# A three-layer kernel with a hand-stored plan: halves of the solved triangle stored apart, two more key buffers, and a plan made anew

## The chip, the core and the metric

The kernel runs on one core of one Trainium2 chip. The metric is the device time of one execution in microseconds (us). The core has TensorE (matrix products; PE in the profile, its weight loads PEld), VectorE (DVE), ScalarE (ACT), GpSimd (POOL) and SyncE (SP), which here does nothing but issue transfers. Each engine works through its own instructions strictly in the order in which they were written, and waits on semaphores for the others.

## What is computed

Three layers on 3072 tokens of 384 channels, cut here to their core. The first is a linear attention whose state is corrected by what it already holds for a key (4 batches, 8 heads, 768 positions, 48 channels per head):

```
k_n = k / (norm(k) + 1e-6)
for t in range(S):
    y[t]  = q[t] @ state
    state = state + beta[t] * outer(k_n[t], v[t] - k_n[t] @ state)
```

The second sends each token with a positive skip score to one of 8 experts and adds gate * relu(x @ w1[e]) @ w2[e]. The third normalises by the root of the mean square and gives (silu(x @ w_gate) * (x @ w_val)) @ w_out.

## The kernel before

The 768 positions are handled in 12 chunks of 64, two to a group (groups 0 to 5); 64 of the partitions hold half of the batches, and a step for one chunk handles the rest in two streams (bp 0 and 1), each with its own state in a PSUM bank (banks 70 and 71 in the order below). Every f32 operand of a product is split into two f16 halves, high and low, and each product is three matmuls (high-high, low-high, high-low).

For each group, `norms` and `prepk` load the keys, normalise and split them (NK), copy them into the order that a turn by DMA needs (four transfers into NB, tag nb, on SP), turn them (KC, a transposing transfer), form the Gram matrices and store them to DRAM (gd). `solve` loads four 32 x 32 blocks per problem from gd, inverts them in 30 steps of two VectorE operations each (tags sm and sa), sets the diagonal (a memset, L271), scales the result (Ts), splits it into halves (Th, Tl) and stores it to DRAM twice, as it is (td) and turned (tn). `merge`, once for each chunk of the group, loads the blocks into W (eight transfers for the group's two chunks from td) and dn (four from tn), and builds the missing block of the 64 x 64 inverse on TensorE (z at L295, x at L310), with ScalarE writing the result into W (x1h, x1l). `prepq` turns the queries and forms their Gram matrix. `step` is the recurrence for one chunk and stream: split the state (Sh on ScalarE, Sl on VectorE with the state's bank as its source), form the residual with it (ks), multiply by W (u), update the state (S), and give the output (yq, y). A step can do ks without W; u needs it.

`Route` then projects each output tile for the experts and scatters the rows; `Rest` decodes and splits the weights of the gated layer, runs the experts and then the gated layer.

The order of the work is not found at run time. `Sched` collects some 3440 operations; `follow` gives each the place, the engine and the buffer slot that stand in three tables, ORDER_, ON_ and SLOT_; `emit` writes them out so. The cost numbers in `dma`, `conv` and the others are those from which a planner made the tables; they are not read when the kernel runs.

The interleaved layout of before: td is [block, problem, row, column, half], so that the high and the low of an element lie side by side, and W keeps that in its last axis.

Of the kernel before, what the change touches and what calls it, by code (L numbers as in the profile page):

```python
# [104 lines left out]
B,H,S,D=4,8,768,48  # L105
# [13 lines left out]
class Base:  # L119
# [58 lines left out]
class Attn(Base):  # L178
# [19 lines left out]
    def norms(s,g):  # L198
        nc=s.nc; sm=lambda: s.small.buf([32])
        n2=sm(); s.ksrc=[]  # L200
        for hf in range(2):
            kf=s.pk.buf([2,HD]); s.ksrc.append(kf)
            s.dma(lambda kf=kf: kf.ap,lambda hf=hf: s.I['kn'][g,hf].rearrange("p (q e)->p q e",q=2),393216,[],[kf],tag="ldk")
# [15 lines left out]
    def prepk(s,g):  # L219
# [3 lines left out]
        for hf in range(2):  # L223
# [7 lines left out]
            for u in range(2):  # L231
                for bp in range(2):
                    s.dma(lambda u=u,bp=bp,NB=NB: NB.ap[UH[bp],:,:,u].rearrange("p l h d->p (l h) d"),lambda u=u,bp=bp,NK=NK: NK.ap[UH[u],bp].rearrange("p l h d->p (l h) d"),260000,[NK],[(NB,(u,bp))],tag="nb")
            s.dma(lambda KC=KC: KC.ap.rearrange("p l h t->p (l h) t"),lambda NB=NB: NB.ap.rearrange("p l h u d->p (l h u d)"),524288,[NB],[KC],tag="trk",kind="t")
# [8 lines left out]
            s.dma(lambda hf=hf: gd.ap[:,16*hf:16*hf+16],lambda gs=gs: gs.ap.rearrange("p q h j->p (q h) j"),524288,[gs],[(gd,hf)],tag="gout")  # L243
# [6 lines left out]
    def solve(s,g):  # L250
# [5 lines left out]
        for b in range(4):  # L256
            half,u=b//2,b%2; r=64*u+32*half
            s.dma(lambda b=b: A.ap[32*b:32*b+32],lambda r=r,half=half: gd.ap[r:r+32,:,32*half:32*half+32].rearrange("i a j->a i j"),262144,[gd],[(A,("l",b))],tag="lda")
# [14 lines left out]
        td=Fixed(s.dram(f"td{g}",[4,32,32,32,2],F16)); tn=Fixed(s.dram(f"tn{g}",[2,32,32,32,2],F16)); s.td[g]=(td,tn)  # L273
        for o in range(2):
            n=(128,64)[o]; Th=s.pTh.buf([32,32,2],F16); src=(lambda: A.ap) if o==0 else (lambda: A.ap[0:64].rearrange("p c i->p i c"))
            s.conv(lambda Th=Th,n=n: Th.ap[0:n,:,:,0],src,1024,[A],[(Th,0)],tag="Th")
            s.tt(lambda Th=Th,n=n: Th.ap[0:n,:,:,1],src,lambda Th=Th,n=n: Th.ap[0:n,:,:,0],ALU.subtract,1024,[A,(Th,0)],[(Th,1)],tag="Tl")
            to=td if o==0 else tn
            s.dma(lambda to=to: to.ap.rearrange("b a r c l->(b a) (r c l)"),lambda Th=Th,n=n: Th.ap[0:n].rearrange("a r c l->a (r c l)"),4096*n,[Th],[to],tag="td")

    def merge(s,g,hf):
# [3 lines left out]
        W=s.pW.buf([2*H,2,32,2],F16); s.W[g,hf]=W; dn=s.pdn.buf([2*H,32,2],F16)  # L285
        R=[[slice(64*u+32*f,64*u+32*f+32) for f in range(2)] for u in range(2)]
        for u in range(2):
            for f in (1,0):
                s.dma(lambda u=u,f=f: W.ap[R[u][f],:,f].rearrange("p a c l->p a (c l)"),lambda u=u,f=f: td.ap[2*f+u,sa].rearrange("a r c l->r a (c l)"),90000,[td],[(W,(f,u))],tag="W")
            s.dma(lambda u=u: dn.ap[R[u][0]].rearrange("p a c l->p a (c l)"),lambda u=u: tn.ap[u,sa].rearrange("a r c l->r a (c l)"),90000,[tn],[(dn,u)],tag="dn")  # L290
        pz=s.ps.buf([2*H,32]); zw=s.pzw.buf([2,2*H,32],F16); fl=lambda a: a.rearrange("p a c->p (a c)")
        def zmm(e,bp):
            for a in range(H*bp,H*bp+H):
                for i,(x,y) in enumerate(((0,0),(1,0),(0,1))):
                    for u in range(2): nc.tensor.matmul(pz.ap[R[u][0],a],GB.ap[R[u][1],x,a],W.ap[R[u][1],a,1,:,y],start=a==0 and i==0,stop=a==2*H-1 and i==2,skip_group_check=True)  # L295
# [22 lines left out]
    def prepq(s,g,q):  # L318
        nc=s.nc; hf,bp=q//2,q%2
        if bp==0:  # L320
            qv=s.pqv.buf([2,2*HD])
            s.dma(lambda: qv.ap,lambda: s.I['qv'][g,hf].rearrange("p (x e)->p x e",x=2),786432,[],[qv],tag="ldq")
# [9 lines left out]
            s.dma(lambda: QC.ap.rearrange("p l h t->p (l h) t"),lambda: NQ.ap.rearrange("p l h d->p (l h d)"),524288,[NQ],[QC],tag="trq",kind="t")  # L332
# [27 lines left out]
    def step(s,g,q,QC,Pt):  # L360
# [19 lines left out]
        s.prod(lambda u,h: pu.ap[u,h],lambda u,l,h: W.ap[u,H*bp+h,:,:,l].rearrange("p f c->p (f c)"),rt,True,True,[W],Rh,pu,[Uh],"u")  # L380
# [141 lines left out]
class Rest(Base):  # L522
# [72 lines left out]
    def moe(s,S):  # L595
        nc=s.nc
        for e in range(E):
# [5 lines left out]
            s.dma(lambda xT=xT: xT.ap.rearrange("p b l k t->p (b l k) t"),lambda xh=xh: xh.ap.rearrange("p b l d->p (b l d)"),393216,[xh],[xT],tag="trx",kind="t")  # L603
# [24 lines left out]
    def glu(s):  # L628
        nc=s.nc
        t0=0  # L630
        for st,N in enumerate(GROUPS):
# [17 lines left out]
            for b in range(N):  # L649
# [3 lines left out]
                s.dma(lambda xT=xT,b=b: xT.ap[:,b].rearrange("p l k t->p (l k) t"),lambda xh=xh: xh.ap.rearrange("p l d->p (l d)"),196608,[xh],[(xT,b)],tag="trn",kind="t")  # L653
# [137 lines left out]
ORDER_=[21,17,33,24,36,168,226,6,9,19,81,34,20,22,35,18,1,37,3,5,4,38,2,169,0,23,14,7,39,170,8,29,12,30,227,10,40,13,41,80,11,25,42,228,26,171,43,16,238,44,32,28,264,45,172,27,46,173,31,47,  # L791
# [90 lines left out]
```

## Time and profile before

| | us |
|---|---|
| median of 3 runs | 1117.39 (1116.77 to 1117.95) |
| the profiled execution, its own time | 1119.22 |
| its span, first to last instruction | 1117.5 |
| busy: TensorE / VectorE / ScalarE | 873.7 / 654.1 / 376.0 |
| mean granted TensorE clock, share of full | 0.826 |

The span falls into attention (to about 505 us), the wait for the experts (to 528), the experts (to 661), a second wait (to 682) and the gated layer. TensorE is nearly always busy in the experts and the gated layer, at a granted clock of 0.98 to 0.99; in attention it works at 0.58 to 0.76, with pauses. Busy times of matmuls are modelled at their ends. A wait is put down to the one that ended last.

### The profile page before, as it was taken

What the parts mean: (1) busy time and instruction counts of PE and PEld (TensorE: products, weight loads), DVE (VectorE), ACT (ScalarE), POOL (GpSimd) and SP (SyncE); (2) the same over time, 40 slices, a digit from 0 to 9 for tenths busy, and PEclk for the clock granted to TensorE, in tenths of its full rate; (3) what the DMA queues carried; (4) which work ended last, traced back from release to release, by engine and by line L of the source; (5) the groups of instructions that cost most, each with busy time, mean ns of one, the idle gap of its engine ahead of it and who ended that gap; (6) DMA issues with size and microseconds to landing.
All of it is one profiled execution on the core that took longest, in us unless ns stands there. A gap on an engine that the chain in (4) does not pass through costs nothing.

```text
span 1117.5 us, 31866 instructions
## 1 busy us (share of the span) xinstructions
PE 873.7 (78%) x14102; PEld 596.9 (53%) x14102; DVE 654.1 (59%) x1511; ACT 376.0 (34%) x707; POOL 64.0 (6%) x83
## 2 busy tenths in 40 slices
PE   0320775975887769681999965999999999999996
PEld 0320564764775657561777745865454444545553
DVE  6458756677566666759989998753424353331230
ACT  3221343461534424451545415643131221111100
POOL 5000001001001010011000012211000000000000
PEclk9955576675666867665999986999999999999998
DMA  9992577386674851765899755531120101000000
GB/s 273 194 218 76 107 147 157 80 171 112 118 137 145 174 109 55 194 198 167 226 289 298 217 164 161 129 89 47 23 70 1 28 2 29 29 1 22 22 15 31
DMA packets 233154, 132.00 MB, mean 118 GB/s; under 512 B 199038, under 2 KB 214995, under 8 KB 233010
## 3 DMA queue, kind: packets, MB, share of 16 engines
q1 hardware_dynamic: 229938, 122.83, 45.1%
q0 software_dynamic: 3072, 7.07, 2.2%
q8 instruction: 112, 1.84, 0.7%
q14 instruction: 32, 0.26, 0.1%
HBM read 74.04 MB, written 31.46 MB: 94 GB/s over the span
## 4 chain that ended last, share of the span: by engine, by line
PE 60%; DMA 11%; DVE 10%; issue 8%; SPq 6%; ACT 4%; another core or an unknown queue 0%; POOL 0%; POOLq 0%; ACTq 0%; DVEq 0%
PE bank L160 14%; PE bank L166 8%; PE bank L168 8%; PE bank L167 8%; SPq L152 6%; PE bank L676 4%; PE bank L674 4%; PE bank L675 4%; DVE arena L136 3%; ACT arena L128 3%; DVE arena L134 3%; DMA arena<-in_w_dram 3%; DMA arena<-arena 3%; PE bank L310 2%; DMA arena<-yd,arena 1%
## 5 line engine op out<-in xcount | busy, mean ns | idle before, releaser
L134 DVE TENSOR_TENSOR arena<-arena 128x512 f16<-128x512 f32 (+20 forms) x558 | 257.7, 472 | 58.4 <-ACT arena L128 25.6
L160 PE MATMUL bank<-arena 64*64 64x48 f16 (+1 forms) x7776 | 197.5, 212 | 102.8 <-DMA arena<-arena 63.5
L166 PE MATMUL bank<-arena 128*128 128x512 f16 (+2 forms) x768 | 236.7, 316 | 42.0 <-DMA arena<-arena 39.2
L160 PEld LDWEIGHTS <-arena 64*64 64x64 f16 x7776 | 183.1, 134 | 132.5 <-issue 65.7
L167 PE MATMUL bank<-arena 128*128 128x512 f16 (+2 forms) x768 | 236.8, 316 | 0.2 <-issue 0.2
L168 PE MATMUL bank<-arena 128*128 128x512 f16 (+2 forms) x768 | 236.7, 316 | 0.0
L128 ACT ACTIVATE arena<-bank 128x384 f16<-128x384 f32 (+4 forms) x258 | 129.6, 529 | 312.5 <-PE bank L676 98.8
L128 ACT ACTIVATE arena<-arena 128x512 f16<-128x512 f32 (+6 forms) x187 | 138.4, 756 | 161.5 <-DVE arena L136 30.4
L136 DVE SCALAR_TENSOR_TENSOR arena<-arena 128x768 f16<-128x768 f32 (+4 forms) x163 | 136.8, 855 | 47.2 <-ACT arena L128 36.4
L136 DVE SCALAR_TENSOR_TENSOR arena<-arena,bank 128x512 f32<-128x512 f32 (+2 forms) x96 | 52.7, 552 | 148.7 <-PE bank L168 111.9
L167 PEld LDWEIGHTS <-arena 128*128 128x128 f16 x768 | 76.5, 100 | 88.9 <-issue 43.0
L664 ACT ACTIVATE arena<-bank 128x512 f32<-128x512 f32 (+2 forms) x96 | 46.2, 488 | 168.3 <-PE bank L168 127.4
L166 PEld LDWEIGHTS <-arena 128*128 128x128 f16 x768 | 76.5, 100 | 46.3 <-issue 0.3
L168 PEld LDWEIGHTS <-arena 128*128 128x128 f16 x768 | 76.5, 100 | 46.2 <-issue 0.3
L674 PE MATMUL bank<-arena 128*128 128x384 f16 x288 | 93.9, 326 | 0.0
L675 PE MATMUL bank<-arena 128*128 128x384 f16 x288 | 93.9, 326 | 0.0
L676 PE MATMUL bank<-arena 128*128 128x384 f16 x288 | 93.9, 326 | 0.0
L129 DVE CAST arena<-arena 128x512 f16<-128x512 f32 (+2 forms) x69 | 28.8, 417 | 58.1 <-PE bank L675 36.6
L295 PE MATMUL bank<-arena 32*32 32x32 f16 x1152 | 22.0, 183 | 42.9 <-DMA arena<-td 30.0
L517 POOL DMA_INDIRECT xs<-arena x24 | 24.4, 1017 | 475.5 <-DMA arena<-td 171.8
L136 DVE SCALAR_TENSOR_TENSOR arena<-bank,arena 128x256 f16<-128x256 f32 (+1 forms) x86 | 37.9, 453 | 13.7 <-ACT arena L128 11.4
L619 PE MATMUL bank<-arena 128*128 128x384 f16 x128 | 41.7, 326 | 2.7 <-DVE arena L130 1.4
(113 smaller groups left out, 735.8 us busy)
## 6 DMA issues: line engine op xcount, KB each, us to landing
arena<-in_w_dram SPq DMA_DIRECT2D x24, 512.0 KB
arena<-in_w_dram SPq DMA_DIRECT2D x32, 384.0 KB
arena<-in_qv_dram SPq DMA_DIRECT2D x12, 768.0 KB
arena<-arena SPq DMA_DIRECT2D x48, 128.0 KB
gd<-arena SPq DMA_DIRECT2D x12, 512.0 KB
arena<-in_kn_dram SPq DMA_DIRECT2D x12, 384.0 KB
xd<-arena SPq DMA_DIRECT2D x12, 384.0 KB
arena<-in_wg_dram SPq DMA_DIRECT2D x9, 512.0 KB
```

The costliest lines, as they stand in the source:

```text
L128: if e is s.nc.scalar: e.activation(out(),in_(),AF.Copy,scale=sc)
L134: return s.sch.op(alts,lambda e: e.tensor_tensor(out(),a(),b(),op=op),r=r,w=w,tag=tag,prio=prio)
L136: return s.sch.op([("DVE",0.07+n*0.00104,port)],lambda e: e.scalar_tensor_tensor(out(),a(),sc() if callable(sc) else sc,b(),op0=op0,op1=op ...
L152: else: fn=lambda e: e.dma_start(out(),in_())
L160: for u in UH: nc.tensor.matmul(o(u),l(u),r(u),start=first and i==0,stop=last and i==n-1,skip_group_check=True)
L166: nc.tensor.matmul(out,lh,rh,start=first,stop=False,skip_group_check=True)
L167: nc.tensor.matmul(out,ll,rh,start=False,stop=False,skip_group_check=True)
L168: nc.tensor.matmul(out,lh,rl,start=False,stop=last,skip_group_check=True)
L664: s.act(lambda e,sg=sg,pp=pp: e.activation(sg.ap,pp[0].ap,AF.Silu,scale=2.0**-7),T,[pp[0]],[sg],table="silu",tag="silu")
L674: nc.tensor.matmul(po.ap,hT.ap[:,f,0,bs],s.wo.ap[:,0,c],start=f==0,stop=False)
L675: nc.tensor.matmul(po.ap,hT.ap[:,f,0,bs],s.wo.ap[:,1,c],start=False,stop=False)
L676: nc.tensor.matmul(po.ap,hT.ap[:,f,1,bs],s.wo.ap[:,0,c],start=False,stop=f==11)
```

## The change

Three things. First, td, tn, Th, W and dn keep the high and the low half apart: in W the axes are now [problem, half, block, column], so that 32 columns of one half lie together. Matmuls and conversions read and write them without a stride; a load of W from td now moves runs of 32 f16 (64 bytes), 1024 of them, where it moved 512 runs of 128 bytes; a load of dn keeps its 128-byte runs. Second, KC (turned keys) and NK (normalised keys) have six slots each instead of five, and one more buffer is zeroed at the start. Third, the sizes and issue times of transfers in the planner's costs are other numbers, and the three tables are other tables, so that the order of the instructions differs nearly everywhere.

```diff
-        return s.sch.op([("SP",1.8 if kind=="t" else 0.46,0)],fn,r=r,w=w,kind=kind,nb=nb,tag=tag,prio=prio)
+        return s.sch.op([("SP",0.7+nb*1.6e-6 if kind=="t" else {"lda":0.61,"W":0.53,"nb":0.73}.get(tag,0.45),0)],fn,r=r,w=w,kind=kind,nb=nb,tag=tag,prio=prio)
...
-        td=Fixed(s.dram(f"td{g}",[4,32,32,32,2],F16)); tn=Fixed(s.dram(f"tn{g}",[2,32,32,32,2],F16)); s.td[g]=(td,tn)
+        td=Fixed(s.dram(f"td{g}",[4,32,2,32,32],F16)); tn=Fixed(s.dram(f"tn{g}",[2,32,32,2,32],F16)); s.td[g]=(td,tn)
...
-        W=s.pW.buf([2*H,2,32,2],F16); s.W[g,hf]=W; dn=s.pdn.buf([2*H,32,2],F16)
+        W=s.pW.buf([2*H,2,2,32],F16); s.W[g,hf]=W; dn=s.pdn.buf([2*H,2,32],F16)
...
-                s.dma(lambda u=u,f=f: W.ap[R[u][f],:,f].rearrange("p a c l->p a (c l)"),lambda u=u,f=f: td.ap[2*f+u,sa].rearrange("a r c l->r a (c l)"),90000,[td],[(W,(f,u))],tag="W")
+                s.dma(lambda u=u,f=f: W.ap[R[u][f],:,:,f].rearrange("p a l c->p (a l) c"),lambda u=u,f=f: td.ap[2*f+u,sa].rearrange("a l r c->r (a l) c"),250000,[td],[(W,(f,u))],tag="W")
...
-        o=lambda l: W.ap[:,:,1,:,l]
+        o=lambda l: W.ap[:,:,l,1]
...
-ORDER_=[21,17,33,24,36,168,226,6,9,19,81,34,20,22,35,18,1,37,3,5,4,38,2,169,0,23,14,7,39,170,8,29,12,30,227,10,40,13,41,80,11,25,42,228,26,171,43,16,238,44,32,28,264,45,172,27,46,173,31,47,
...
-SLOTS={}
+SLOTS={'KC':6,'NK':6}
```

Where the order moves, at the three places that the prediction speaks of. On VectorE, the end of solve 1 before the change. A row 128x27x4 is a product of step 27 of the solve's 30, the rows between with one size are its additions, and the row from bank_71 is Sl, the split of the second stream's state for chunk 2:

```order
L136 SCALAR_TENSOR_TENSOR arena<-bank_71,arena 128x384
L134 TENSOR_TENSOR arena<-arena 128x2x8x48
L134 TENSOR_TENSOR arena<-arena 128x27x4
L129 COPY arena<-bank_69 128x512
L134 TENSOR_TENSOR arena<-arena 128x84
L134 TENSOR_TENSOR arena<-bank_65,arena 128x512
L134 TENSOR_TENSOR arena<-arena 128x28x3
```

And the end of the same solve now, where L271 is the memset behind step 30 and the row from bank_70 is Sl of the first stream for chunk 2:

```order
L134 TENSOR_TENSOR arena<-arena 128x58
L134 TENSOR_TENSOR arena<-bank_69,arena 128x512
L134 TENSOR_TENSOR arena<-arena 128x29x2
L134 TENSOR_TENSOR arena<-arena 128x30 x2
L271 MEMSET arena 128x32
L134 TENSOR_TENSOR arena<-arena 128x1024
L136 SCALAR_TENSOR_TENSOR arena<-bank_70,arena 128x384
```

Before, both splits for chunk 2 stand inside the solve (the first five rows further up); now the solve ends ahead of both, and only the two splits for chunk 1 stand inside it. The same holds of solve 2 with chunk 4; in solves 4 and 5 one of the two splits of chunks 8 and 10 stood inside before and none now; solve 3 had none before and has none now.

On SP, around the store of solve 1 (td_79) and the loads of W from it, before (64x16x64 are the copies nb ahead of a turn, gd_81 and gd_84 the Gram matrices of groups 2 and 3):

```order
L151 DMA_TRANSPOSE arena<-arena 128x16x128 x2
L152 DMA td_79<-arena 128x2048
L152 DMA arena<-gd_81 32x32x32 x4
L152 DMA tn_80<-arena 64x2048
L152 DMA arena<-td_79 32x16x64 x8
L152 DMA gd_84<-arena 128x1024
L152 DMA arena<-tn_80 32x16x64 x4
```

And now:

```order
L152 DMA td_79<-arena 128x2048
L152 DMA arena<-gd_81 32x32x32 x4
L152 DMA tn_80<-arena 64x2048
L152 DMA arena<-in_qv_dram 128x1536
L152 DMA arena<-arena 64x16x64 x4
L152 DMA arena<-in_kn_dram 128x768
L152 DMA gd_84<-arena 128x1024
L152 DMA arena<-td_79 32x32x32 x2
L152 DMA arena<-tn_80 32x16x64 x2
L152 DMA arena<-td_79 32x32x32 x4
```

Seven transfers more stand between the store tn_80 and the first load of W, whose shape has changed to 32x32x32.

On SP, ahead of the first loads of gd (gd_75, group 0's), before:

```order
L152 DMA arena<-arena 64x16x64 x8
L152 DMA gd_75<-arena 128x1024 x2
L152 DMA arena<-in_kn_dram 128x768 x2
L151 DMA_TRANSPOSE arena<-arena 128x16x128 x3
L152 DMA arena<-gd_75 32x32x32 x4
```

And now:

```order
L152 DMA arena<-in_kn_dram 128x768
L152 DMA arena<-in_qv_dram 128x1536
L151 DMA_TRANSPOSE arena<-arena 128x16x128
L152 DMA arena<-arena 64x16x64 x4
L152 DMA gd_75<-arena 128x1024
L152 DMA arena<-arena 64x16x64 x4
L152 DMA gd_75<-arena 128x1024
L152 DMA arena<-in_kn_dram 128x768 x2
L151 DMA_TRANSPOSE arena<-arena 128x16x128 x3
L152 DMA arena<-gd_75 32x32x32 x4
```

The two key loads ahead of the three turns are group 2's before and group 3's now; group 2's have moved further up.

## Rows read from the trace of the kernel before

**Rows 1.** The page's part 4: the chain that ended last, by engine.

```profile
PE 60%; DMA 11%; DVE 10%; issue 8%; SPq 6%; ACT 4%; another core or an unknown queue 0%; POOL 0%; POOLq 0%; ACTq 0%; DVEq 0%
```

**Rows 2.** Windows by stage: length, busy us (x instructions) per engine, clock, DMA share.

```profile
0.00:115.75 115.75, 19.90 (x676) 18.14 (x677) 71.38 (x140) 27.02 (x36) 14.13 (x35) 0.74 0.85 190
115.75:186.68 70.93, 51.93 (x1812) 43.00 (x1814) 49.62 (x135) 31.85 (x56) 0.00 (x0) 0.64 0.68 133
186.68:265.29 78.61, 55.71 (x1804) 45.73 (x1803) 50.71 (x136) 33.56 (x57) 8.11 (x8) 0.63 0.66 135
265.29:334.80 69.51, 59.27 (x1905) 48.44 (x1902) 45.91 (x111) 30.77 (x54) 0.00 (x0) 0.62 0.58 114
334.80:399.48 64.68, 45.94 (x1610) 38.07 (x1607) 40.50 (x117) 26.49 (x48) 4.09 (x4) 0.76 0.65 151
399.48:461.03 61.55, 51.32 (x1736) 40.78 (x1736) 43.22 (x120) 23.08 (x42) 3.89 (x4) 0.67 0.44 101
461.03:505.50 44.47, 35.69 (x1015) 29.13 (x1016) 25.79 (x59) 23.37 (x42) 3.89 (x4) 0.58 0.62 195
505.50:528.24 22.74, 0.28 (x6) 0.21 (x5) 20.86 (x70) 2.31 (x4) 4.42 (x4) 0.50 0.54 165
528.24:661.35 133.11, 128.84 (x960) 95.29 (x960) 126.78 (x236) 64.72 (x125) 0.00 (x0) 0.98 0.83 245
...
681.98:1117.50 435.52, 424.79 (x2592) 238.13 (x2591) 161.71 (x352) 108.08 (x235) 19.81 (x19) 0.99 0.15 40
```

**Rows 3.** Windows from a group's later split to the next z; sum of four first halves.

```profile
155.00:186.68 31.68, 19.66 (x507) 16.67 (x501) 20.11 (x59) 12.59 (x20) 0.00 (x0) 0.61 0.81 170
233.71:265.29 31.58, 16.76 (x483) 15.09 (x482) 21.43 (x60) 11.15 (x16) 3.89 (x4) 0.61 0.92 176
315.33:334.80 19.47, 17.38 (x452) 14.55 (x451) 12.58 (x37) 5.51 (x11) 0.00 (x0) 0.59 0.87 141
388.92:399.48 10.56, 4.47 (x166) 3.71 (x161) 7.34 (x27) 1.59 (x4) 0.00 (x0) 0.90 0.77 131
441.72:461.03 19.31, 12.89 (x494) 10.32 (x493) 15.80 (x36) 8.42 (x14) 0.00 (x0) 0.85 0.73 165
...
sum 193.43, PE 160.74 PEld 129.36 DVE 123.20 ACT 87.22 POOL 12.21; mean PE 40.18 PEld 32.34 DVE 30.80 ACT 21.80 POOL 3.05
```

**Rows 4.** VectorE in order of time: start, length, operation, [idle before, releaser].

```profile
83.77 19.45 DVE L134 TENSOR_TENSOR arena<-arena 128x130 f32<-128x130 f32 x51
...
136.31 0.56 DVE L136 SCALAR_TENSOR_TENSOR arena<-bank,arena 128x384 f16<-128x384 f32 x1 [0.50 <-ACT arena L128]
...
155.15 0.56 DVE L136 SCALAR_TENSOR_TENSOR arena<-bank,arena 128x384 f16<-128x384 f32 x1 [1.03 <-ACT arena L128]
...
160.28 0.69 DVE L129 COPY arena<-bank 128x512 f32<-128x512 f32 x1 [3.26 <-PE bank L160]
...
169.35 0.09 DVE L271 MEMSET arena<- 128x32 f32 x1
```

**Rows 5.** SP's issues in order of time: start, length of all, operation, count.

```profile
59.97 2.49 SPq L152 DMA_DIRECT2D arena<-in_kn_dram  x2
...
181.62 4.62 SPq L152 DMA_DIRECT2D arena<-td  x8
...
186.82 2.69 SPq L152 DMA_DIRECT2D arena<-tn  x4
```

**Rows 6.** Groups by line and form, ScalarE from PSUM: count, busy us, mean ns.

```profile
L128 ACT ACTIVATE arena<-bank 128x512 f16<-128x512 f32 x24 | 17.7, 739 | 32.5 <-PE bank L310 19.4 <-PE bank L315 7.7 <-remote 5.5
...
L128 ACT ACTIVATE arena<-bank 128x512 f32<-128x512 f32 x20 | 11.8, 594 | 44.2 <-PE bank L160 44.2
```

**Rows 7.** Transfers of L152: issue on SP, ns least/median/most.

```profile
L152 SPq DMA_DIRECT2D arena<-arena x48: 590/826/3097, 21.8 to 363.6; - x48
L152 SPq DMA_DIRECT2D arena<-td x48: 430/494/2012, 112.9 to 455.2; - x48
L152 SPq DMA_DIRECT2D arena<-gd x24: 319/616/1867, 71.6 to 390.6; - x24
```

More of the change, by code (lines that the diff above doesn't have):

```diff
@@ L202, in norms @@
             kf=s.pk.buf([2,HD]); s.ksrc.append(kf)
-            s.dma(lambda kf=kf: kf.ap,lambda hf=hf: s.I['kn'][g,hf].rearrange("p (q e)->p q e",q=2),393216,[],[kf],tag="ldk")
+            s.dma(lambda kf=kf: kf.ap,lambda hf=hf: s.I['kn'][g,hf].rearrange("p (q e)->p q e",q=2),415000,[],[kf],tag="ldk")
             sq=s.psq.buf([16,D])
@@ L232, in prepk @@
                 for bp in range(2):
-                    s.dma(lambda u=u,bp=bp,NB=NB: NB.ap[UH[bp],:,:,u].rearrange("p l h d->p (l h) d"),lambda u=u,bp=bp,NK=NK: NK.ap[UH[u],bp].rearrange("p l h d->p (l h) d"),260000,[NK],[(NB,(u,bp))],tag="nb")
-            s.dma(lambda KC=KC: KC.ap.rearrange("p l h t->p (l h) t"),lambda NB=NB: NB.ap.rearrange("p l h u d->p (l h u d)"),524288,[NB],[KC],tag="trk",kind="t")
+                    s.dma(lambda u=u,bp=bp,NB=NB: NB.ap[UH[bp],:,:,u].rearrange("p l h d->p (l h) d"),lambda u=u,bp=bp,NK=NK: NK.ap[UH[u],bp].rearrange("p l h d->p (l h) d"),306000,[NK],[(NB,(u,bp))],tag="nb")
+            s.dma(lambda KC=KC: KC.ap.rearrange("p l h t->p (l h) t"),lambda NB=NB: NB.ap.rearrange("p l h u d->p (l h u d)"),880000,[NB],[KC],tag="trk",kind="t")
             for bp in range(2):
@@ L257, in solve @@
             half,u=b//2,b%2; r=64*u+32*half
-            s.dma(lambda b=b: A.ap[32*b:32*b+32],lambda r=r,half=half: gd.ap[r:r+32,:,32*half:32*half+32].rearrange("i a j->a i j"),262144,[gd],[(A,("l",b))],tag="lda")
+            s.dma(lambda b=b: A.ap[32*b:32*b+32],lambda r=r,half=half: gd.ap[r:r+32,:,32*half:32*half+32].rearrange("i a j->a i j"),306000,[gd],[(A,("l",b))],tag="lda")
         bn=sm(); s.ts(lambda: bn.ap,btg,-1.0/256,None,ALU.mult,None,32,[bt],[bn])
@@ L294, in zmm @@
                 for i,(x,y) in enumerate(((0,0),(1,0),(0,1))):
-                    for u in range(2): nc.tensor.matmul(pz.ap[R[u][0],a],GB.ap[R[u][1],x,a],W.ap[R[u][1],a,1,:,y],start=a==0 and i==0,stop=a==2*H-1 and i==2,skip_group_check=True)
+                    for u in range(2): nc.tensor.matmul(pz.ap[R[u][0],a],GB.ap[R[u][1],x,a],W.ap[R[u][1],a,y,1],start=a==0 and i==0,stop=a==2*H-1 and i==2,skip_group_check=True)
         for bp in range(2): s.ped(lambda e,bp=bp: zmm(e,bp),24,32,[GB,(W,(1,0)),(W,(1,1))]+([pz] if bp else []),[pz],also=[zw],tag="z")
@@ L304, in w2 @@
             for l in range(2):
-                for u in range(2): r=R[u][1]; nc.tensor.matmul(fl(px.ap[r]),s.c.idp.ap[r,r],W.ap[r,:,1,:,l],start=l==0,stop=False,skip_group_check=True)
+                for u in range(2): r=R[u][1]; nc.tensor.matmul(fl(px.ap[r]),s.c.idp.ap[r,r],W.ap[r,:,l,1],start=l==0,stop=False,skip_group_check=True)
         s.ped(w2,2,512,[(W,(1,0)),(W,(1,1)),s.c.idp],[px],also=[W],tag="w2")
@@ L309, in xmm @@
                 for i,(x,y) in enumerate(((0,0),(1,0),(0,1))):
-                    for u in range(2): r=R[u][0]; nc.tensor.matmul(px.ap[r,a],dn.ap[r,a,:,x],zw.ap[r,y,a],start=a==0 and i==0,stop=False,skip_group_check=True)
+                    for u in range(2): r=R[u][0]; nc.tensor.matmul(px.ap[r,a],dn.ap[r,a,x],zw.ap[r,y,a],start=a==0 and i==0,stop=False,skip_group_check=True)
         for bp in range(2): s.ped(lambda e,bp=bp: xmm(e,bp),24,32,[dn,zw,px],[px],tag="x1")
-        o=lambda l: W.ap[:,:,1,:,l]
+        o=lambda l: W.ap[:,:,l,1]
         K1=[(W,(1,0)),(W,(1,1))]
@@ L321, in prepq @@
             qv=s.pqv.buf([2,2*HD])
-            s.dma(lambda: qv.ap,lambda: s.I['qv'][g,hf].rearrange("p (x e)->p x e",x=2),786432,[],[qv],tag="ldq")
+            s.dma(lambda: qv.ap,lambda: s.I['qv'][g,hf].rearrange("p (x e)->p x e",x=2),840000,[],[qv],tag="ldq")
             vf=lambda: qv.ap[:,1].rearrange("p (q e)->p q e",q=2)
@@ L331, in prepq @@
             QC=s.pQC.buf([2,H,128],F16); s.QC[g,hf]=QC
-            s.dma(lambda: QC.ap.rearrange("p l h t->p (l h) t"),lambda: NQ.ap.rearrange("p l h d->p (l h d)"),524288,[NQ],[QC],tag="trq",kind="t")
+            s.dma(lambda: QC.ap.rearrange("p l h t->p (l h) t"),lambda: NQ.ap.rearrange("p l h d->p (l h d)"),880000,[NQ],[QC],tag="trq",kind="t")
         QC=s.QC[g,hf]; KC=s.KC[g,hf]; bs=UH[bp]; pp=s.ps.buf([H,C]); pm=s.ppm.buf([H,C])
@@ L379, in step @@
         pu=s.ps.buf([H,D]); Uh=s.pUh.buf([2,HD],F16)
-        s.prod(lambda u,h: pu.ap[u,h],lambda u,l,h: W.ap[u,H*bp+h,:,:,l].rearrange("p f c->p (f c)"),rt,True,True,[W],Rh,pu,[Uh],"u")
+        s.prod(lambda u,h: pu.ap[u,h],lambda u,l,h: W.ap[u,H*bp+h,l].rearrange("p f c->p (f c)"),rt,True,True,[W],Rh,pu,[Uh],"u")
         puf=lambda: pu.ap.rearrange("p h d->p (h d)")
@@ L866 @@
+SLOT_=[0,3,2,1,5,4,0,1,2,3,0,5,4,1,0,0,0,0,1,0,1,2,0,0,0,0,0,2,3,0,1,1,1,1,5,2,1,0,3,0,0,0,1,0,0,2,0,3,0,0,0,0,4,0,0,2,0,1,0,2,0,0,1,3,1,1,3,1,5,0,1,0,1,1,5,0,4,1,1,0,1,4,0,1,0,0,0,2,1,4,1,2,1,2,5,1,0,1,1,1,
[15 rows of a table added]
 PLAN=(ORDER_,ON_,SLOT_)
-SLOTS={}
+SLOTS={'KC':6,'NK':6}
 def kernel(q,k,v,beta,moe_w_skip,moe_w_gate,moe_w1,moe_w2,moe2_w_gate,moe2_w_val,moe2_w_out,moe2_rms_g):
```

22 lines of the change are left out of this document (11 added, 11 removed), and 144 rows, old and new, of tables (ORDER_, SLOT_).

## The prediction

> **What bounds the kernel now.** I read the windows cut by stage first, then the instructions of VectorE and of the DMA queue in order of time, then the groups by line and form. The chain of waits [rows 1] is 60% TensorE, 11% DMA and 10% VectorE, so no engine alone sets the end; it has to be read by stage. [Rows 2] cuts the span at 115.75 us, where the first merge product z starts, at the start of z for each later group (for group 3, whose z ran early and whose x products waited, at its x), and at the ends of the stages. The experts (528.24 to 661.35) have TensorE busy 128.84 of 133.11 us, the gated layer 424.79 of 435.52: TensorE sets both, and the change takes no matmul away. The hole of 22.74 us between attention and experts is one chain (rank, scatter, load, split, turn). What is left is attention, 505.5 us. Its opening is 115.75 us with TensorE busy for 19.90 of them. The five periods behind it take 70.93, 78.61, 69.51, 64.68 and 61.55 us, 345.28 in all, with TensorE busy 264.17 (77%) and VectorE 229.96 (67%). A stage in which nothing is full waits for a chain.
>
> That chain is the recurrence with the solve in it. A period has two halves: from z until the state is split (Sl) for the group's next even chunk, and from that split until the next z. In the four first halves that I cut (186.68 to 233.71, 265.29 to 315.33, 334.80 to 388.92, 399.48 to 441.72) TensorE is busy 160.74 of 193.43 us, 83.1%; in the five second halves 71.16 of 112.60, 63% [rows 3] (both are the sums of its five window rows). The second half is where TensorE waits for the solved triangle. VectorE shows why [rows 4]: the split of chunk 1 is done at 136.3 + 0.56 us, the split of chunk 2 at 155.15, and the end of solve 1 (the memset, L271) comes only at 169.35. The solve's last steps stand in VectorE's order behind that second split and behind a copy out of PSUM that waits 3.26 us for TensorE. From the memset it is another 17.3 us to z at 186.68; W is issued from 181.62 [rows 5].
>
> **The change part by part.** *The order.* On VectorE the memset of solves 1 and 2 now stands ahead of both splits of the next even chunk, where it stood behind both; in solves 4 and 5 it stands ahead of both where it stood behind one; solve 3 was ahead already. So the solve waits for a state that is one chunk older, about 19 us in group 1 (136.3 against 155.15). After that split, 18 VectorE rows remain to the memset; in solve 0, which nothing interrupts, 51 such rows took 19.45 us [rows 4], so 7 us: the memset would come at some 144 us rather than 169. W then lies on SP behind seven rows more than before, four turn copies at 0.83 us and three that I take at the 0.49 of a W load [rows 7], so 17.3 + 4.8 = 22 us from the memset to z: W is there at about 166 us, 20 earlier. But TensorE has 19.66 us of work of its own between the split of chunk 2 and z [rows 3]; from 155.7 and at 83.1% that ends at 179. TensorE is the next to be late, and the gain of group 1 is not 20 us but 8. I count all groups so: TensorE runs through the second halves at the share that it reaches in the first halves, 71.16 / 0.831 = 85.6 us instead of 112.6, **-27.0 us** (by group -8.0, -11.4, +1.4, -5.2, -3.8: most of it where the order moved most, nothing in group 3). The ends: 0, if another wait takes its place, and -49.5, if all five periods reach the share of the densest stretch shown, 17.38 / 19.47 = 89.3% (264.17 / 0.893 = 295.8 against 345.3). I take -27 since it uses a share that this kernel already holds for 193 us.
>
> *The opening.* SP issues without a pause here, and ahead of the first gd loads two more key loads stand (group 3's). Two such loads took 2.49 us of the queue [rows 5]: +2.5. The first query loads now go ahead of the first key loads; the bound is their 1.57 MB at the 190 GB/s of the opening [rows 2], 8.3 us, the other end 0, as the same transfers were in flight together before. I take +1, near zero, since the first turn waits for the query split in both orders. Sum **+3.5**, ends 0 and +11. The zeroing of the sixth key buffer is one operation more in this stretch on an engine that is not on this chain: nothing, at most one memset.
>
> *The halves apart: ScalarE and VectorE.* The write of a merge's result, x1h and x1l, was a strided f16 write of 739 ns; the same size and source written contiguously took 594 ns [rows 6]. Twenty-four of them give 3.5 us of ScalarE; on the chain are the two of each group's first half, 12 x 0.145 = **-1.7**. The Th and Tl splits after each solve lose the same stride; I bound them by the same 0.145 us each, two on the chain per group, -1.7 more, and count 0, since the second pair still reads across the triangle. Matmuls that read W contiguously: 0; no row tells the two layouts apart. Here a page speaks against the gain: the Trainium skill, "SBUF — State Buffer", section "Door 1: The DMA port swizzle", says that a stride is free as long as accesses fall at least twice into a 16-byte line, which a stride of 4 bytes does. By it this edit would give 0 and the sum would be 1.7 us later; the 145 ns between the two rows disagree, if the stride is their only difference.
>
> *The halves apart: loads of W.* A load moves the same 64 KB in 1024 runs of 64 bytes instead of 512 of 128. Its issue took 494 ns (median) before; a load with 1024 runs took 616 (gd) or 826 (turn copies) [rows 7]. 48 loads: +5.9 to +15.9 us of SP; below zero is excluded, since no run gets longer. Four issues stand ahead of what the first z of a group needs: 24 x 0.122 = **+2.9**; the end is all 48 at 0.332, +15.9. I take the gd price, as it is a load from DRAM of the same shape.
>
> *Buffers and rates.* The sixth slots for turned keys and for their norms cost nothing in time but let group 3's keys be turned earlier; that is in the order above. The new transfer rates are read by no instruction. In the experts and the gated layer the orders differ by single rows; I count 0, ends -3 and +5, as VectorE there is busy 126.78 of 133.11 us and a stall shows at once.
>
> Sum: -27.0 + 3.5 - 1.7 + 2.9 = **-22.3 us**. The profiled execution took 1119.22 us (span 1117.5 and 1.7 around it), which is 1.83 above the median of the three runs, 1117.39. So 1096.9 for such an execution, **1095** for the median.
>
> **The rivals.** *TensorE fills up.* The solve stops being the limit in every period, and TensorE runs at 89.3%: -49.5 + 3.5 - 1.7 + 2.9 = -44.8, 1073. For it: by the walk above W is there before TensorE asks, in group 1 by 13 us. Against: VectorE would be at 230 / 296 = 78% in strict order, and some of its operations still wait for TensorE inside the solve.
>
> *The gain is given back on SP.* W now waits behind turn copies that wait for a split on VectorE, so z comes no earlier, and the density of the second halves stays at 63%: 0 + 3.5 - 1.7 + 2.9, **1122**. For it: in group 1 seven issues stand newly between tn and W. Against: the memset itself comes some 25 us earlier, five times the 4.8 us that they cost.
>
> *Slower: the 64-byte runs.* Each group waits for eight loads of W that now cost the 826 ns of the turn copies, and the order gains nothing since SP sets the period: 3.5 + 15.9 - 1.7 = +17.7, **1135**. It decides once W comes later than TensorE's own work ahead of z ends: in group 1 the walk above leaves 13 us for that (166 against 179), in group 3, whose memset stays where it was, next to nothing. For it: the runs are twice as many, and before, eight W issues took 4.62 us and four of dn 2.69 more [rows 5], on a queue that also holds the turn copies. Against: gd loads of 1024 runs cost 616. A page bears on it: the Trainium skill, "DMA: Bandwidth & Descriptors", section "Specifications", says that runs under 512 bytes are below line rate, as they are read, modified and written. [...]
>
> **How the numbers follow.** Forecast (1083 to 1110): 0.51. TensorE fills up (under 1083): 0.22. Given back on SP (1111 to 1123): 0.15. The short runs (about 1135): 0.12. The range reaches from 1068, the second case with the opening at 0, to 1123; it leaves out some 0.07 below and 0.12 above. A measurement of this kernel tells about 0.2% from no change, 1115.2 to 1119.6. Faster: 0.51 + 0.22 + 0.04 of the third case = 0.77; same 0.06; slower 0.05 + 0.12 = 0.17.
>
> **What would show it.** In the profile after: the second memset of L271 near 147 us (opening included) and ahead of the split of chunk 2; z of group 1 near 182 (179 and the opening) instead of 186.68; TensorE at 80 to 85% over the five periods; the end of attention near 483 instead of 505.5; td loads near 0.62 us of issue each; the f16 write of 128x512 from PSUM near 0.59 us. The forecast is wrong if the memsets come earlier and z does not, if the opening grows by more than 6 us, or if the time from 528.24 on moves by more than 5.

## The result, and the profile after

The changed kernel took 1101.26 us (median of 3, 1097.35 to 1109.57) where the kernel before took 1117.39: a ratio of 0.9866, 95% interval 0.9818 to 0.9914, or 16 us less. The forecast was 1095 with a range of 1068 to 1123. The profiled execution is the longest of the three, 1109.57 us with a span of 1107.8, 9.7 us less than the span before.

The windows of the changed kernel, cut as [rows 2] are (length, busy us per engine, granted clock, DMA share, GB/s; the third and the fifth period are cut at x, as there):

```profile
0.00:121.33 121.33, 20.74 (x772) 18.57 (x773) 83.34 (x159) 25.89 (x35) 13.97 (x35) 0.78 0.89 198
121.33:182.26 60.93, 50.05 (x1694) 41.57 (x1694) 42.31 (x99) 29.78 (x52) 0.00 (x0) 0.67 0.70 131
182.26:257.91 75.65, 59.91 (x1811) 49.69 (x1810) 49.52 (x137) 30.70 (x55) 4.17 (x4) 0.59 0.73 136
257.91:335.24 77.33, 58.87 (x1912) 49.02 (x1911) 49.25 (x144) 30.72 (x56) 4.25 (x4) 0.63 0.70 137
335.24:392.70 57.46, 47.15 (x1612) 38.75 (x1612) 38.82 (x100) 22.19 (x40) 3.89 (x4) 0.74 0.51 110
392.70:455.46 62.76, 51.15 (x1737) 41.38 (x1736) 43.17 (x125) 27.90 (x51) 3.89 (x4) 0.66 0.53 125
455.46:504.00 48.54, 39.71 (x1025) 32.81 (x1022) 26.48 (x86) 21.05 (x39) 5.71 (x6) 0.50 0.46 157
504.00:521.94 17.94, 0.00 (x1) 0.00 (x0) 16.00 (x42) 4.55 (x6) 2.32 (x3) 0.50 0.62 178
521.94:653.64 131.70, 129.03 (x960) 95.31 (x960) 126.85 (x236) 65.72 (x124) 0.00 (x0) 0.97 0.84 252
...
672.85:1107.80 434.95, 424.94 (x2592) 238.32 (x2591) 154.57 (x333) 116.61 (x251) 20.33 (x19) 0.99 0.17 40
```

Against [rows 2], stage by stage: opening +5.6 us; the five periods 334.13 instead of 345.28, -11.2 (by group -10.0, -3.0, +7.8, -7.2, +1.2); from the last cut to the experts 66.48 instead of 67.21, -0.7; experts -1.4; the stretch between the experts and the gated layer 19.21, -1.4; gated layer -0.6. TensorE is busy 267.13 of the 334.13 us, 80%, against 77%. (The chain of waits, [rows 1], breaks off after one step in this execution and can't be read.)

The periods divided at the later split of the even chunk, as in [rows 3], at 165.92, 230.79, 317.49, 381.29 and 439.14: the sum of the five second halves, then that of the four first halves.

```profile
sum 88.94, PE 74.74 PEld 65.61 DVE 53.57 ACT 26.59 POOL 0.00; mean PE 14.95 PEld 13.12 DVE 10.71 ACT 5.32 POOL 0.00
...
sum 200.60, PE 155.03 PEld 124.85 DVE 135.29 ACT 90.91 POOL 16.21; mean PE 38.76 PEld 31.21 DVE 33.82 ACT 22.73 POOL 4.05
```

The second halves are 23.7 us shorter (112.60 before) and TensorE is busy in 84% of them, not 63%. The first halves are longer: these four by 7.2 us (193.43 before) and at 77% instead of 83%, the first group's by 5.3 (44.59 instead of 39.25). TensorE's work in all five is the same, 192.4 us after and 193.0 before.

VectorE at the end of solve 1, which answers [rows 4]: the memset now ends the solve ahead of both splits of chunk 2.

```profile
151.53 0.09 DVE L271 MEMSET arena<- 128x32 f32 x1
...
152.79 0.55 DVE L136 SCALAR_TENSOR_TENSOR arena<-bank,arena 128x384 f16<-128x384 f32 x1
...
165.92 0.55 DVE L136 SCALAR_TENSOR_TENSOR arena<-bank,arena 128x384 f16<-128x384 f32 x1
```

SP behind it, which answers [rows 5]: from the store of td (the first row) to the first load of W are 14.5 us, in which the four turn copies alone take 4.1.

```profile
156.93 0.34 SPq L152 DMA_DIRECT2D td<-arena  x1
...
166.03 4.11 SPq L152 DMA_DIRECT2D arena<-arena  x4
...
171.47 2.20 SPq L152 DMA_DIRECT2D arena<-td  x2
```

The memset is 17.8 us earlier than before and z of group 1 only 4.4 (182.26). It does not wait for W there: TensorE works on its own products right up to it, and no idle time stands ahead of z.

```profile
179.84 2.50 PE L470 MATMUL bank<-arena 128*128 128x9 f32 x11
182.26 1.38 PE L295 MATMUL bank<-arena 32*32 32x32 f16 x90
```

The issue of W loads (least, median, most ns) and ScalarE's write of 128x512, which answer [rows 7] and [rows 6]:

```profile
L152 SPq DMA_DIRECT2D arena<-td x48: 375/670/5503, 117.3 to 445.9; - x48
```

```profile
L128 ACT ACTIVATE arena<-bank 128x512 f16<-128x512 f32 x24 | 14.3, 594 | 23.1 <-PE bank L310 17.5 <-PE bank L315 3.9 <-DMA arena<-arena 1.5
```

### The profile page after: what moved, and what is told of

Read it like the earlier page. It is cut to its first block, busy times and chain, and to the rows that moved or that the text cites. A ratio compares the mean times of both kernels' runs of the same rounds, so it can differ in the third digit from the quotient of the medians.

```text
span 1107.8 us, 31869 instructions
## 1 busy us (share of the span) xinstructions
PE 881.6 (80%) x14102; PEld 605.4 (55%) x14102; DVE 647.1 (58%) x1497; ACT 379.7 (34%) x718; POOL 65.8 (6%) x83
## 5 line engine op out<-in xcount | busy, mean ns | idle before, releaser
L134 DVE TENSOR_TENSOR arena<-arena 128x512 f16<-128x512 f32 (+22 forms) x558 | 257.9, 470 | 84.9 <-ACT arena L128 67.9
L160 PE MATMUL bank<-arena 64*64 64x48 f16 (+1 forms) x7776 | 202.0, 212 | 114.0 <-DMA arena<-arena 69.5
L160 PEld LDWEIGHTS <-arena 64*64 64x64 f16 x7776 | 185.4, 135 | 147.9 <-issue 75.8
L128 ACT ACTIVATE arena<-bank 128x384 f32<-128x384 f32 (+4 forms) x256 | 127.0, 514 | 320.9 <-PE bank L676 96.5
L128 ACT ACTIVATE arena<-arena 128x512 f16<-128x512 f32 (+6 forms) x204 | 148.6, 740 | 159.0 <-DVE arena L136 46.1
L129 DVE CAST arena<-arena 128x512 f16<-128x512 f32 (+4 forms) x50 | 21.3, 425 | 41.5 <-PE bank L675 32.8
L636 POOL DMA_INDIRECT arena<-yd,arena x24 | 27.5, 1148 | 257.9 <-DVE arena L130 147.8
```

The costliest lines, as they stand in the source:

```text
L128: if e is s.nc.scalar: e.activation(out(),in_(),AF.Copy,scale=sc)
L134: return s.sch.op(alts,lambda e: e.tensor_tensor(out(),a(),b(),op=op),r=r,w=w,tag=tag,prio=prio)
L160: for u in UH: nc.tensor.matmul(o(u),l(u),r(u),start=first and i==0,stop=last and i==n-1,skip_group_check=True)
```

## The experiments

The experiments ran in three sets of four kernels, each beside the kernel before, which took 1107.09, 1106.95 and 1119.70 us in them. So times are compared as ratios to the kernel before of the same set, with 95% intervals, and 0.001 is 1.1 us.

**The changed kernel again.**

> The changed kernel again, unchanged, to see how wide its own times are (its three executions were 1097.35, 1101.26 and 1109.57 us, those of the kernel before lay within 1.2 us). If the 12 us between them are a property of the new order (a race between transfers and the queue's issues that falls one way or the other), they appear again, and a profile of a short execution differs from that of the long one in one or two stages of attention. If they were an accident of that chip, the times lie within 3 us around 1100. The forecast of 1095 stays right in the first case only if the short executions are the more frequent ones.

0.9822 (0.9786 to 0.9857), 1087.92 us, 1084.83 to 1091.29. The width, 6.5 us, is smaller than the 12 us of the first three, though not 3. The profiled execution was a short one (span 1083.1), with attention over at 483.4 us. In its last stretch the same matmuls took:

```profile
441.50:483.42 41.92, 32.93 (x1023) 27.19 (x1021) 26.35 (x85) 20.70 (x39) 6.28 (x6) 0.62 0.54 183
```

This is 6.8 us of TensorE less than the 39.71 in the stretch from 455.46 above, for two matmuls fewer, at a granted clock of 0.62 instead of 0.50 (0.50 is the lower of the two levels throughout). In the period ahead of it TensorE had been busy much alike, 51.15 of 62.76 us and 49.09 of 59.16. So a third of the 20.6 us by which attention differs between the two executions goes with the clock in one stretch. One profile of this kernel says little about 10 us.

The five periods take 319.3 us in e0, with TensorE busy for 259.3 of them (81%). The kernel before has no profile in this set, in which it was 10 us shorter too.

**The layout alone, and the plan alone.** In e1 the layout lines of the diff are put into the kernel before, whose tables stay; in e2 they are taken back in the changed kernel:

```diff
-        W=s.pW.buf([2*H,2,2,32],F16); ...
+        W=s.pW.buf([2*H,2,32,2],F16); ...
-        o=lambda l: W.ap[:,:,l,1]
+        o=lambda l: W.ap[:,:,1,:,l]
...
```

> The kernel before with the halves stored apart and nothing else: its own three tables, five slots. My sum gives +2.9 for the issue of W and -1.7 for the unstrided writes of ScalarE, +1.2 us: no difference that can be told (1117 to 1121). The rival of the short runs gives +14 to +18 us. A third theory, that the layout is worth something where the sum has none (matmuls and weight loads that read W without a stride, the splits of the solved triangle), gives -3 to -8 us. In the profile: the f16 write of 128x512 from PSUM by ScalarE at 594 ns instead of 739, issue of td loads at 616 ns median instead of 494.

> The changed kernel with the halves interleaved as before: new tables and six slots, old layout. If the order brings the gain, it keeps it: 1099 to 1102 us where the changed kernel has 1101 (my sum puts the layout at +1.2 on its side, so this one would be 1 us earlier). If the layout brings it, this one lies at 1112 or later. With e1 the two parts should add up; if they don't, the new order needs the cheaper or dearer loads of the new layout.

The layout alone: 1.0092 (1.0059 to 1.0124), 10 us slower, between my +1.2 and the rival's +14 to +18. The plan alone: 0.9745 (0.9709 to 0.9781), 28 us faster. In the same set the changed kernel had 0.9822, so in the new plan too the layout costs 8.5 us. What it was to give came as expected: the f16 write takes 738 ns in e2 and 594 in e1 and e0. The issue of W is longer with it, e1 first, then e2:

```profile
L152 SPq DMA_DIRECT2D arena<-td x48: 430/672/2226, 111.9 to 456.7; - x48
```

```profile
L152 SPq DMA_DIRECT2D arena<-td x48: 433/490/3390, 117.4 to 426.9; - x48
```

0.18 us more, 8.7 us over 48 loads. TensorE's waits that the profile puts down to W and dn are longer too (line waited for: us, times, longest). In e1 from 110 to 510 us:

```profile
PE bank L295 <- DMA arena<-td: 33.4, 4, 22.6
...
PE bank L305 <- DMA arena<-td: 8.2, 6, 4.0
PE bank L310 <- DMA arena<-tn: 7.1, 6, 3.1
```

48.7 us in these three lines; the kernel before, with the same tables, has 30.0 + 6.1 + 4.4 = 40.5 there. (The wait of some 22 us in both is the first z, in the opening.) This does not show where the 10 us went, though. The two profiled executions are from different sets and took nearly the same time, 1117.71 and 1119.22 us, and the idle time ahead of z that the profile puts down to nothing is 5.1 us in e1 and 12.8 before, which nearly cancels the difference.

**The order of VectorE, and the stores behind it.** The kernel before; in groups 1 and 2 the split of the triangle and its two stores on SP go ahead as well. At the end of solve 1, and likewise of 2, 4 and 5:

```diff
+L134 TENSOR_TENSOR arena<-arena 128x29x2
+L134 TENSOR_TENSOR arena<-arena 128x30 x2
+L271 MEMSET arena 128x32
+L134 TENSOR_TENSOR arena<-arena 128x1024
 L136 SCALAR_TENSOR_TENSOR arena<-bank_70,arena 128x384
...
-L271 MEMSET arena 128x32
```

> The kernel before (old layout, five slots, old engines) with one thing moved: on VectorE the last steps of solves 1, 2, 4 and 5, with the memset and the scaling, stand ahead of the first split of the next even chunk, as they do in the changed kernel, and in groups 1 and 2 the split and the stores of the triangle right behind the second split. Nothing else of the new plan. The forecast's term for the order, -27 us, was for this mechanism: if it is right, most of the gain of the changed kernel (-10 to -16 us here) comes with this move alone, the opening staying at 115.75. If the rest of the new plan brings the gain, this one is within 4 us of the kernel before; if the later split of the state costs as much as the earlier solve gives, it is as late or later.

1.0004 (0.9974 to 1.0035): nothing. VectorE did as told:

```profile
151.53 0.09 DVE L271 MEMSET arena<- 128x32 f32 x1
```

SP gave it back. td is stored at 159.62, 16.5 us earlier than before, but W waits its turn behind key loads, copies and turns for later groups:

```profile
159.62 0.33 SPq L152 DMA_DIRECT2D td<-arena  x1
...
171.49 4.61 SPq L151 DMA_TRANSPOSE arena<-arena  x2
176.15 3.72 SPq L152 DMA_DIRECT2D arena<-gd  x4
179.92 5.35 SPq L152 DMA_DIRECT2D arena<-td  x8
```

z of group 1 starts at 185.86, 0.8 us earlier than before. In between TensorE waits 5.1 us for a turn and 1.4 and 1.1 for W. This is the rival "given back on SP", in the old plan.

**The order of SP as well.** e4, with W ahead of those transfers:

```diff
 L152 DMA td_79<-arena 128x2048
 L152 DMA tn_80<-arena 64x2048
+L152 DMA arena<-td_79 32x16x64 x8
+L152 DMA arena<-tn_80 32x16x64 x4
 L152 DMA arena<-in_kn_dram 128x768
...
-L152 DMA arena<-td_79 32x16x64 x8
```

> The kernel before with the moved solves of the run e4_order, and on SP the loads of W and dn of groups 1 to 5 now directly behind the two stores of the triangle instead of behind the transfers for later groups (13, 12, 1, 5 and 2 issues less ahead of them). In e4 the memset of solve 1 came at 151.5 us and z all the same at 185.9, as W was issued only from 179.9: in theory the queue gave the gain back. Then this one brings z of group 1 to 170 to 178, and 8 to 20 us in all over the kernel before. If instead TensorE's own work or the recurrence sets z, z stays at 180 or later and the time within 4 us of the kernel before; if the turned keys of later groups, which now go out later, are what is missed, the time rises.

1.0149 (1.0106 to 1.0192): slower, though W was issued by 167.4. z came at 189.1. I put that down to the row rank that stands ahead of z on TensorE, and moved z ahead of it too. But the trace of e5 has the 7.45 us of idle TensorE far ahead of rank, at the product L462, and none at z:

```profile
176.10 0.90 PE L462 MATMUL bank<-arena 128*128 128x128 f32 x3 [7.45 <-ACT arena L128]
```

The move:

```diff
+L305 MATMUL (w2), L295 MATMUL (z), L299 MATMUL (zwlp)
 L499, L498 MATMUL (rank)
-L305 MATMUL (w2), L295 MATMUL (z), L299 MATMUL (zwlp)
```

> The kernel of e5_order_w (earlier solves on VectorE, earlier W on SP, 1.0149 of the kernel before) with one thing more, on TensorE and ScalarE: z and the first steps behind it (zwlp, in group 1 also w2 and x of the first chunk) of groups 1 and 2 stand ahead of the product rank (L499), which waits for VectorE's routing rows, and not behind it. In e5 W of group 1 was issued by 167.4, and z came at 188.8 all the same, 7.5 us of idle TensorE in between, as it stood in TensorE's order behind rank. If the gain of an order is had only when all queues on the chain are moved (VectorE, SP, TensorE), z of group 1 comes at 170 to 178 and the whole is 10 to 25 us shorter than e5, 0.992 to 1.005 of the kernel before. If something else in the old order holds the recurrence (turned keys that now go out later), it stays at 1.010 or more.

1.0159 (1.0114 to 1.0204): nothing gained, and the trace shows what holds z of group 1 in both. SP now issues a key load for group 4 at 170.65, behind W, where it was issued at 162.89 in e4:

```profile
170.65 0.43 SPq L152 DMA_DIRECT2D arena<-in_kn_dram  x1
```

ScalarE has the square of these keys next in its order (10.90 us idle), VectorE its sum (10.20), and TensorE the product L462, whose operand ScalarE copies behind the square. In order of engine, each with its wait:

```profile
174.52 0.84 ACT L205 ACTIVATE arena<-arena 128x768 f32<-128x768 f32 x1 [10.90 <-DMA arena<-in_kn_dram]
```

```profile
175.39 0.95 DVE L206 TENSOR_REDUCE arena<-arena 128x16 f32<-128x768 f32 x1 [10.20 <-ACT arena L205]
```

```profile
175.79 0.90 PE L462 MATMUL bank<-arena 128*128 128x128 f32 x3 [9.27 <-ACT arena L128]
...
190.05 1.46 PE L295 MATMUL bank<-arena 32*32 32x32 f16 x96
```

A load that nobody needs for three groups stopped three engines, since their orders were made for the place that it had had. That this is the whole 1.5% is not shown: no run put the load back ahead of W.

**W earlier in the new plan.** The changed kernel, and (e6) the kernel e2, with this in groups 1 to 3, in e6 in group 5 too (group 2 shown):

```diff
 L152 DMA tn_83<-arena 64x2048
+L152 DMA arena<-td_82 32x32x32 x8
+L152 DMA arena<-tn_83 32x16x64 x4
 L152 DMA arena<-arena 64x16x64 x4
 L152 DMA arena<-in_kn_dram 128x768
...
-L152 DMA arena<-td_82 32x32x32 x4
```

> The changed kernel with one thing moved on SP: in groups 1, 2 and 3 the loads of W and dn stand directly behind the stores of the triangle, ahead of the copies for the turn, the key and query loads and the store of the Gram matrix (7, 7 and 5 issues). In the profile of the changed kernel W of group 2 was issued from 240.28, 13.8 us after the store of td at 226.51, and TensorE waited 16 us for it. If the queue holds W up, this gives 5 to 15 us; if the transfers themselves or TensorE's own work set z, less than 3 us.

> The new plan with the interleaved layout (the run e2_plan, 0.9745 of the kernel before), and the loads of W and dn of groups 1, 2, 3 and 5 directly behind the stores of the triangle. If the gain of the layout's removal (runs of 128 bytes again) and that of the earlier W are independent, this is the sum of both: 0.960 to 0.970. If both are the same gain (W comes earlier either way, and then TensorE is the limit), it stays at 0.972 to 0.976.

e3: 0.9810 (0.9768 to 0.9852) where the changed kernel had 0.9822: no difference that can be told. z of group 1 came 8.5 us earlier (175.8 against 184.3 in e0), x 0.9 (190.1 against 191.0). TensorE's wait has moved on, to the next thing that is late; from 172 to 195 us, e3 and then e0:

```profile
PE bank L499 <- DVE arena L494: 11.3, 1, 11.3
```

```profile
PE bank L499 <- DVE arena L494: 3.6, 1, 3.6
```

There was no wait for W to take away. The 16 us that the expectation of e3 names are the first z, in the opening; here is the changed kernel from 110 to 510 us, where the kernel before has 30.0:

```profile
PE bank L295 <- DMA arena<-td: 17.2, 2, 16.1
```

The other 1.1 us are at the first z too. Behind the first merge (from 131 us on) TensorE waits for no transfer until attention ends, in the changed kernel, e0, e2, e3 and e6 alike.

e6: 0.9722 (0.9682 to 0.9762), beside 0.9745 for e2: again not to be told apart. It beats both kernels. It differs from e3 of the same set in the layout and in group 5's loads: 0.0088, 9.7 us, in line with the 8.5 and 10.2 of the layout. The issue of W has a median of 565 ns in e3 and 488 in e6, which is 3.7 us over 48 loads, so here it does not account for the 9.7.

**The start of VectorE.** The changed kernel, with the zeroings and one scaling (the first row) behind the first splits:

```diff
-L139 TENSOR_SCALAR arena<-arena 128x3
-L37 COPY bank_66<-arena 128x512
...
 L130 TENSOR_SCALAR arena<-arena 128x16x48
...
+L139 TENSOR_SCALAR arena<-arena 128x3
+L37 COPY bank_66<-arena 128x512
```

> The changed kernel with one thing moved on VectorE, at the start: a scaling of three columns, the four zeroings of PSUM banks and the two of key buffers stand behind the splits of group 0's queries and keys instead of ahead of them. In the profile of the changed kernel the scaling of 128x3 took 2.97 us and the copy behind it 3.49, up to the end of GpSimd's memsets at 15.3, and the first turn was issued at 21.9 us against 17.3 in the kernel before, while SP from there on issued without a pause. If this start is where the opening lost its 5.6 us, the first turn comes at 17 to 19 us, the first z 3 to 5 us earlier, and the whole is 2 to 5 us shorter. If the loads of group 3's keys ahead of the first Gram loads are the reason, as I had it (2.5 us), the first z moves by less than 1 us.

0.9785 (0.9739 to 0.9832), the first z at 117.7 instead of 122.2. In the changed kernel the scaling, the copies and GpSimd's memsets stand so:

```profile
12.51 2.97 DVE L139 TENSOR_SCALAR arena<-arena 128x3 f32<-128x3 f32 x1
12.58 4.67 DVE L37 COPY bank<-arena 128x512 f32<-128x512 f32 x3
```

```profile
9.15 6.30 POOL L35 MEMSET arena<- 128x1024 f32 x7
```

```profile
21.88 4.15 SPq L151 DMA_TRANSPOSE arena<-arena  x1
```

The last row is the first turn, behind which SP issues without a pause. In e9 it comes as early as in the kernel before, and the scaling takes 0.16 us:

```profile
17.27 4.44 SPq L151 DMA_TRANSPOSE arena<-arena  x1
```

So the late start of the opening lay there. Whether its 4.6 us reach the end is unclear, since the intervals of e9 and e0 overlap. The same edit on e6:

> The new plan with the interleaved layout and the earlier W (the run e6_plan_w, 0.9722), and the zeroings at the start behind the first splits on VectorE (as in e9_open, which took the first z from 122.2 to 117.5 us and some 4 us of the whole). If the parts add up: 0.966 to 0.970, 1069 to 1074 us where the kernel before has 1107.

0.9738 (0.9696 to 0.9780), first z at 115.8, and no better than e6. Both beat the changed kernel, by intervals that do not touch, and their difference can't be told.

**Short runs where nothing waits at once.**

```diff
-tn=Fixed(s.dram(f"tn{g}",[2,32,32,32,2],F16))
+tn=Fixed(s.dram(f"tn{g}",[2,32,2,32,16,2],F16))
```

> The kernel e11_best with one thing changed: tn lies in DRAM with the two halves of a row's columns apart, so that the 24 loads of dn move 1024 runs of 64 bytes where they moved 512 of 128; W, its loads and what the matmuls read stay as they are. In the traces the issue of a load of td took 490 ns at 512 runs and 664 to 672 at 1024. If the 64-byte runs are what the layout of the changed kernel cost (8 to 11 us over 48 loads), half as many loads cost 3 to 6 us here, with the issue of tn loads at 600 to 700 ns instead of 490. If that cost lay elsewhere (the writes and reads of the halves), this kernel is within 2 us of e11_best.

0.9735 (0.9697 to 0.9774), the same as e11. Here 24 loads had 64-byte runs, and their issue took 564 ns instead of 487. That is 1.8 us in all, less than intervals of some 4 us to either side can show, so this run neither shows nor excludes a cost of short runs. (Loads of dn had 554 ns in e1 and 563 in e0 as well, where their runs stay at 128 bytes, so the length of the runs is not all that the issue depends on.) No run changed W's runs alone.

**The kernel before in the third set.**

> The kernel before, unchanged, for a profile on the same chip as the other runs of this call: 1105 to 1110 us here, with its first z at 115 and its five periods at 330 to 345 us. It tells how much of the 10 us between the two chips' times of this kernel lies in attention (expected: nearly all, in the granted clock and the waits of TensorE) and gives the rows to compare the others with.

1118.70 us, as in the first table, with the first z at 115.0; not 1105 to 1110, since the kernel before was longer throughout this set. It decides nothing beside the ratios.

## Why the prediction was right, and where it was not

The total was right, the mechanism for it only in part, and two terms were wrong in opposite directions: the plan gave 28 us (e2) for the 23.5 of the order and the opening, and the layout took 8.5 to 10 for 1.2. That the sum comes as close as it does is partly luck.

**The second halves** came out as a sum: 88.9 us against 85.6 foreseen, at 84% busy against 83.1%. By group they did not: -15.3, -4.5, -1.7, +0.9 and -3.0 us, where I had -8.0, -11.4, +1.4, -5.2 and -3.8. In group 1 part of it is the cut itself: the later split comes 10.8 us later (of which the opening has 5.6), which shortens the second half and lengthens the first. What held there is the end: the memset ahead of the split, z at 182.26 for 182, and TensorE at work right up to z, as I had it.

**The first halves** are the step that failed. I held them fixed, and they grew by 12.5 us (by group +5.3, +1.5, +9.5, -8.1 and +4.2) for the same work of TensorE. So in this execution the order gave -11 in the periods, with the dearer loads in it, and not -27. Why they grew is open. A solve that goes ahead of a split can push the split back, which would fit group 1, but the largest growth is in group 3, where no solve moved past a split: there the second half lost 1.7 us, where I had +1.4 more, and the whole period grew by 7.8. In e0 the periods come to 319.3 us, -26 against the profile before, but no profile of the kernel before stands beside that execution.

**The cause** was named too narrowly. The wait that I named is gone: in the kernel before TensorE waited, behind the first merge, 16.1 us for W and dn (7.6 at z, 6.1 at L305, 2.4 at x) and 6.9 for turned keys, and in the changed kernel and e2 for neither. But the moves that I argued from do not bring this about. Run e4 made them; TensorE still waited 18.8 us for W and dn and 10.7 for turned keys, and nothing was gained. e5 moved SP too, the waits for W and dn fell to 0.4 us, and the time rose by 1.5% all the same, since TensorE stood still elsewhere; e10 moved TensorE's order and gained nothing more. The plan as a whole, which moves every queue and has the two more buffers, gives 28 us (e2). Which part of it brings the 28 is not settled; what is shown is that the move I named doesn't, by itself.

**The layout** was the term most wrong: +2.9 for four issues a group and -1.7 for ScalarE, +1.2; measured +10.2 and +8.5 alone, and +9.7 with group 5's loads moved. The issue is 670 ns, not 616, and all 48 loads issue 8.7 us longer, where I had counted four a group. That this is how the layout costs its 8 to 10 us is not shown: in the new plan TensorE waits for no load of W behind the opening, and between e3 and e6 the issue differs by 3.7 us only. The unstrided write is as priced, 594 ns, and buys nothing that could be seen beside that.

On the two pages of the Trainium skill: "SBUF — State Buffer", section "Door 1: The DMA port swizzle", counts a stride of 4 bytes as free; e2 and e0 differ in the layout alone and the write takes 738 against 594 ns, so it is not free here. For "DMA: Bandwidth & Descriptors", section "Specifications", which puts runs under 512 bytes below line rate, both layouts lie below that size, and the time from issue to landing of a W load went from 3.5 us (e2) to 4.1 (e0).

**The opening** was +5.6 for +3.5. The two key loads fit what I said: from the first turn to the first gd load are 54.4 us before and 56.5 after, 2.1 more for the 2.5 (1.1 came back behind it). The other 4.6 us are the later first turn, 21.88 instead of 17.27, which I bounded by transfers; it was VectorE's order (e9). I had counted the one zeroing more as nothing; what cost time was where the zeroings and the scaling stand, ahead of the first splits.

**Experts and gated layer** were counted 0, with ends -3 and +5, and gave -1.4 and -0.6; with the stretch between them the time from the experts' start to the end is 3.4 us shorter. "Single rows" was not true, though: VectorE's casts of 128x512 went from 56 to 35 and ScalarE's from 59 to 80,

```profile
L129 DVE CAST arena<-arena 128x512 f16<-128x512 f32 x35 | 15.1, 432 | 41.1 <-PE bank L675 32.8 <-PE bank L160 7.4
```

most of them in the gated layer. In e0 the experts took 129.5 us, against 133.1 before; why is open.

**The marks.** TensorE at 80% over the periods, at the edge of 80 to 85. Attention over at 504.0, not 483, in this execution (483.4 in e0). **The rivals.** TensorE does not fill up. Given back on SP is what e4 shows. The layout's cost is real, at 10 us instead of 18, and smaller than what the plan brings; that it comes from the short runs is not shown.

## What to carry to other kernels

Here an order gave nothing when parts of it were moved by hand, queue by queue, and 2.5% when all of it was planned anew. So before counting what an earlier step gives, follow its result through each queue to the consumer, and count what is pushed back on each of them. When a change has parts that can be separated, price each by the runs; here one part took back nearly a third of what the other gave, and the best kernel leaves it out.

## What the runs showed of the hardware

VectorE can stand still while GpSimd writes. The scaling of three columns took 2.97 us, up to 15.48, and GpSimd's seven memsets end at 15.45 (9.15 + 6.30); alone it takes 0.16 (e9). The Trainium skill, "SBUF — State Buffer", section "🔬 SBUF: two separate sides", tells of a port pair that these two engines share as an exclusive lock, held for a whole instruction. The trace agrees with a lock, but this one lasted over some three memsets of 0.9 us each. Not every instruction is held: in the kernel before, three copies of 128x512 on VectorE took 0.68 to 0.73 us and a fourth 1.06 beside the same seven memsets (9.24 to 15.61). Which ones are held, these runs do not show.

The same program differed by 12 us between executions of one set; between the two of it that were profiled, in two sets, 6.8 us of TensorE's busy time lay in one stretch, with its granted clock at 0.50 or 0.62.
